# A plan of norm steps for each token block between two layers, and a budget for VectorE's weight conversions

## The chip, the cores and the metric

The kernel runs on one core of one Trainium2 chip. The metric is the device time of one execution in microseconds (us), taken from runs without the profiler; the profile comes from one further execution. Engines are named TensorE (PE in the profile, its weight loads PEld), VectorE (DVE), ScalarE (ACT), GpSimd (POOL) and SyncE (SP, which only issues DMAs here).

## The reference, cut to what matters

Attention over 4 batches, 8 heads, 576 positions and 64 channels, with a learned position bias, gives x of 2304 tokens x 512. Two feed-forward layers follow; the weights arrive as float64.

```python
def _moe_ref(x, w_in, w_out):                 # layer 1, d_ff 2048
    h = x @ w_in
    g = h * np.cos(h)
    return g @ w_out

def _moe2_ref(x, w_gate, w_val, w_out, rms_g):  # layer 2, d_ff 1536
    rms = np.sqrt(np.mean(x * x, axis=-1, keepdims=True) + 1e-06)
    xn = x / rms * rms_g
    g = xn @ w_gate
    silu = g * (1.0 / (1.0 + np.exp(-g)))
    val = xn @ w_val
    return silu * val @ w_out
```

## The kernel before, in words

Attention fills the first 300 us of the profile and is not touched. Then come 140 **items**, numbered n = 0 to 139: 0 to 79 are layer 1, 80 to 139 layer 2. An item is one token block times one slice of 128 hidden units. The tokens lie in five blocks, four of 512 tokens (0, 1, 3, 4) and one of 256 (block 2). Layer 1 has four chunks of four slices, layer 2 four chunks of three; inside a chunk the loop runs over blocks, then slices. In the last chunk of layer 1 (items 60 to 79) and the first of layer 2 (80 to 94) the blocks come in the order 0, 2, 1, 3, 4, so layer 1 ends for block 0 at item 63, block 2 at 67, block 1 at 71, block 3 at 75, block 4 at 79, and layer 2 starts them at items 80, 83, 86, 89 and 92.

Each fp32 product is done as three matmuls of a high and a low part (high x high, high x low, low x high). `run_item(n)` issues in this order: squares and output steps of the norm that are due (ScalarE, GpSimd); the product up of item n (12 matmuls into a PSUM tile `h`, `hg` or `hv`; three such tiles rotate, and the norm's transposes `ssp` and `rbp` use the same three); the activation; the product down of item n-2 (`item_down`, matmuls into `y`, which has five PSUM tiles, four for a block of 512); a tick of the weight pipeline. In layer 1 the activation is three VectorE steps (L653 to L655), Abs and Sin on ScalarE, one VectorE step (L662), a cast on ScalarE (L663) and a subtraction on GpSimd (L664), the last two making the high and low part of `g`, which the product down of item n reads two items later. In layer 2 it is Sigmoid on ScalarE, two VectorE steps (L676, L679), then the cast and the subtraction (L680, L681). When `item_down` ends a chunk of a block, VectorE moves its four `y` tiles to `yacc` (L715, L717: below, the evictions); in two places of the order (`sums_first`) they stand ahead of L662.

Weights pass a pipeline of pieces (512 columns each, two per slice in layer 1, three in layer 2): a DMA of float64, an absolute value on ScalarE (L113), four VectorE operations that make float32 of it (L124, L126, L128, L130: **quarters**; `w_conv` counts them), then a split into high and low (ScalarE L148, GpSimd L149) into a ring of ten. Piece i is called split i below. A split waits until the ring's slot is free, and the number of splits in a tick is one in layer 1 and two in layer 2.

Between the layers each block is normalised: squares (`rms_sq`), three additions of them on VectorE (`rms_add`, L733), a sum by transposes on TensorE (`rms_sum`, L739), the reciprocal root (`rms_mean`: four VectorE operations, L748 to L752, and twelve small GpSimd operations, L754 to L757), transposes back (`rms_back`, L764) and a copy, the multiplication of four parts (`rms_xn`, VectorE L771), and the split into `xh` and `xl` (`rms_out`, ScalarE L776 and GpSimd L777). All engines work through their instructions in program order, so the item at which a step is issued sets what stands behind it.

Of the kernel before, what the change touches and what calls it, by code (L numbers as in the profile page):

```python
# [25 lines left out]
BLKS = [(0, 512), (512, 512), (2048, 256), (1024, 512), (1536, 512)]  # L26
# [3 lines left out]
CH1 = 4  # L30
CH2 = 3
# [7 lines left out]
LAG = 2  # L39
# [5 lines left out]

SMALLPS = {33, 34, 35}
LB = {10: 0, 11: 1, 18: 2, 19: 3, 26: 4, 27: 5}
WF = 2
ORDER2 = [0, 2, 1, 3, 4]

LEAST = 2.0 ** -15
# [3 lines left out]
def attn_moe(tc, qd, kd, vd, smallp, lrow, ident_d, wf1, wf2, rmsg, out):  # L55
# [61 lines left out]
    def w_conv(quarters=2):  # L117
        for _ in range(quarters):
            i = wstate["conv"]
            r = raw_t[i]  # L120
            hi, lo = r[:, :, 1], r[:, :, 0]
            t = w32_t[i]
            if wstate["half"] == 0:
                nc.vector.tensor_scalar(t.bitcast(F32), t.bitcast(F32), LEAST, GREATEST, op0=ALU.max, op1=ALU.min)  # L124
            elif wstate["half"] == 1:
                nc.vector.tensor_scalar(t, t, 3, 0x3FFFFFFF, op0=ALU.logical_shift_left, op1=ALU.bitwise_and)  # L126
            elif wstate["half"] == 2:
                nc.vector.scalar_tensor_tensor(t, hi, -0x40000000, t, op0=ALU.bitwise_and, op1=ALU.bitwise_or)  # L128
            else:
                nc.vector.scalar_tensor_tensor(t, lo, 29, t, op0=ALU.logical_shift_right, op1=ALU.bitwise_or)  # L130
                raw_t.pop(i)
                wstate["conv"] += 1
            wstate["half"] = (wstate["half"] + 1) % 4

    def w_split(eng=nc.gpsimd):
# [13 lines left out]
        eng.tensor_tensor(t[:, 1, :], r, t[:, 0, :].bitcast(F32), op=ALU.subtract)  # L149
        w_t[pieces[i]] = t  # L150
        wstate["split"] += 1

    def w_fill(halves=1):
        for _ in range(halves):
            if wstate["conv"] < wstate["absd"]:
                w_conv()

    def w_tick(can_split, nsplit=1, forward=True):

# [304 lines left out]
    small = ph0.tile([128, 34 + NTT + NR], F32, name="small")  # L464
# [119 lines left out]
    items = []  # L584
# [7 lines left out]
    NI = len(items)  # L592
# [35 lines left out]
    def tasks(n, fns):  # L628
        k = 0
        for fn, *a in later.get(n, ()):  # L630
            if fn in fns:
                fn(*a)
                k += 1
        return k

    def fill(n):
        return tasks(n, (rms_add, rms_mean, rms_xn))

    def item_up(n, between=None, sums_first=False):
        m, c, bi, fi = items[n]  # L640
        t0, tn = BLKS[bi]
        f = c * (CH1 if m == 1 else CH2) + fi
        g = mp.tile([128, 2, 512], F32R, tag="g", name="g", bufs=LAG + 2)
        if n == 0:
            mp.tile([128, 96], F32, name="evenm")
        if m == 1:
            ps = up(w_t[(1, f, 0)], bi, "h")[:, :tn]
            if between is not None:
                between()
            tasks(n, (rms_sum, rms_back))  # L650
            t = mp.tile([128, 512], F32, tag="t", name="t", bufs=2)[:, :tn]
            r = mp.tile([128, 512], F32, tag="r", name="r", bufs=2)[:, :tn]
            nc.vector.tensor_scalar(t, ps, INV2PI, MAGIC, op0=ALU.mult, op1=ALU.add)  # L653
            nc.vector.tensor_scalar(t, t, MAGIC, -TWO_PI, op0=ALU.subtract, op1=ALU.mult)  # L654
            nc.vector.tensor_tensor(r, ps, t, op=ALU.add)  # L655
            if fill(n) < WF:
                w_fill()
            nc.scalar.activation(r, r, AF.Abs)  # L658
            nc.scalar.activation(r, r, AF.Sin, bias=halfpi[:, 0:1], scale=-1.0)

            def end():
                nc.vector.tensor_tensor(t, r, ps, op=ALU.mult)  # L662
                nc.scalar.copy(g[:, 0, :tn], t)  # L663
                nc.gpsimd.tensor_tensor(g[:, 1, :tn], t, g[:, 0, :tn].bitcast(F32), op=ALU.subtract)  # L664


            if sums_first:
                gt[n] = g
                return end
            end()  # L670
        else:
            pg = up(w_t[(2, f, 0)], bi, "hg")[:, :tn]
            tasks(n, (rms_sum, rms_back))
            t = mp.tile([128, 512], F32, tag="t", name="t", bufs=2)[:, :tn]
            nc.scalar.activation(t, pg, AF.Sigmoid)  # L675
            nc.vector.tensor_tensor(t, t, pg, op=ALU.mult)  # L676
            fill(n)
            pv = up(w_t[(2, f, 1)], bi, "hv")[:, :tn]
            nc.vector.tensor_tensor(t, t, pv, op=ALU.mult)  # L679
            nc.scalar.copy(g[:, 0, :tn], t)  # L680
            nc.gpsimd.tensor_tensor(g[:, 1, :tn], t, g[:, 0, :tn].bitcast(F32), op=ALU.subtract)  # L681
        gt[n] = g

    def item_down(n):
        m, c, bi, fi = items[n]
        t0, tn = BLKS[bi]
        ch = CH1 if m == 1 else CH2
        nch = (NF1 if m == 1 else NF2) // ch
        f = c * ch + fi
        g = gt.pop(n)  # L690
        wt = w_t[(m, f, 1 if m == 1 else 2)]
        nd = 4 if m == 1 else tn // 128
        wid = tn if m == 1 else 512
        if fi == 0:
            ypsum[bi] = [env["psY"].tile([128, 512], F32, tag="y", name="y", bufs=5) for _ in range(nd)]
        for d in range(nd):
            ps = ypsum[bi][d][:, :wid]
            w_ = (wt[:, 0, 128 * d:128 * d + 128], wt[:, 1, 128 * d:128 * d + 128], g[:, 0, :tn], g[:, 1, :tn])
            if m == 1:
                mm3(ps, [w_], tn, fi == 0, fi == ch - 1)  # L700
            else:
                gs = slice(128 * d, 128 * d + 128)
                mm3(ps, [(g[:, 0, gs], g[:, 1, gs], wt[:, 0, :], wt[:, 1, :])], 512, fi == 0, fi == ch - 1)
        if fi == ch - 1:
            acc = yacc if m == 1 else oacc
            if c == 0:
                if tn == 512:
                    acc[bi] = env["yp"].tile([128, 4, 512], F32, tag="y", name="yacc", bufs=4)
                else:
                    acc[bi] = env["yp"].tile([128, nd, wid], F32, tag="ys", name="yaccs", bufs=1)  # L710
            a = acc[bi]
            for d in range(nd):
                ps = ypsum[bi][d][:, :wid]
                if c == 0:
                    nc.vector.tensor_copy(a[:, d, :wid], ps)  # L715
                else:
                    nc.vector.tensor_tensor(a[:, d, :wid], ps, a[:, d, :wid], op=ALU.add)  # L717
                if m == 2 and c == nch - 1:
                    nc.sync.dma_start(out[t0 + 128 * d:t0 + 128 * d + 128, :], a[:, d, :])
            if m == 1 and c == nch - 1:  # L720
                return bi
        return None

    rst = {}

# [47 lines left out]
    def rms_out(bi, d):  # L773
# [3 lines left out]
        nc.gpsimd.tensor_tensor(xl[:, d, t0:t0 + tn], t, xh[:, d, t0:t0 + tn].bitcast(F32), op=ALU.subtract)  # L777

    NI1 = NF1 * len(BLKS)
    RMS_AT = (-14, -10, -5, -1, 2)  # L780
    RMS_STEPS = [
        [(rms_sq, 0), (rms_sq, 1)], [(rms_add, 1), (rms_sq, 2), (rms_sq, 3)], [(rms_add, 2), (rms_add, 3)],
        [(rms_sum,), (rms_mean,)], [], [(rms_back,)], [(rms_xn, 0)],
        [(rms_xn, 1), (rms_xn, 2), (rms_out, 0)], [(rms_xn, 3), (rms_out, 1)], [(rms_out, 2), (rms_out, 3)],
    ]
    def ready(i):
        while wstate["split"] <= i:
            if wstate["split"] < wstate["conv"]:
                w_split()
            elif wstate["conv"] < wstate["abs"]:  # L790
                w_conv()
            elif wstate["abs"] < wstate["dma"]:
                w_abs()
            else:
                w_dma()

    def run_item(n, between=None):
        tasks(n, (rms_sq, rms_out))
        end = None
        if n < NI:  # L800
            m, c, bi, fi = items[n]
            ready(pieces.index((m, c * (CH1 if m == 1 else CH2) + fi, m - 1)))
            end = item_up(n, between, n >= LAG and items[n - LAG][3] == CH1 - 1 and 2 in (bi, items[n - LAG][2]))
        d = n - LAG
        if d >= 0:
            m, c, bi, fi = items[d]
            ready(pieces.index((m, c * (CH1 if m == 1 else CH2) + fi, m)))
            bi = item_down(d)
            if bi is not None:
                n0 = NI1 + RMS_AT[ORDER2.index(bi)]  # L810
                for i, x in enumerate(RMS_STEPS):
                    later.setdefault(n0 + i, []).extend((x_[0], bi, *x_[1:]) for x_ in x)
        if end is not None:
            end()
        m, c, bi, fi = items[min(n, NI - 1)]
        w_tick(lambda i: i < WA + WB or n > 1 and (i < RING or lastuse[pieces[i - RING]] <= n - SPL),
               nsplit=2 if n < 6 or m == 2 else 1)
        if m == 2:
            w_fill(2 if n % 2 else 1)

    def rest():
        av(15, 1)
# [89 lines left out]
```

## Time and profile before

| | |
|---|---|
| median of 3 runs | 1155.5 us (1155.28 to 1155.86) |
| profiled execution | 1155.4 us, span 1153.6 us |
| PE busy | 1142.8 us (99%) |
| PEld busy | 919.0 us (80%) |
| DVE busy | 806.9 us (70%) |
| ACT busy | 546.5 us (47%) |
| POOL busy | 443.8 us (38%) |
| granted TensorE clock | 1.000 over the span |

The span runs from the first to the last instruction; 1.8 us of the execution lie outside it. A share is of the whole span, so an engine with a low share can still be full in one stretch. Matmuls are pipelined and their ends are modelled: the time from one start to the next tells more than the time of one.

### The profile page before, as it was taken

Reading aid. Unit: us, or ns where it says so; the run is one execution under the profiler, and the core shown is the slowest. Engines: PE = TensorE matmul, PEld = TensorE weight load, DVE = VectorE, ACT = ScalarE, POOL = GpSimd, SP = SyncE. Lnnn points to the kernel's source line nnn. Section 1 sums busy time; section 2 is a strip of 40 time slices with the busy share of each in tenths; the row PEclk is TensorE's granted clock in tenths of the full one; section 3 lists DMA queues with packets and bytes.
Section 4 is the critical chain, followed back from the end, with each engine's and each line's share of the span. In section 5 each row is a group of like instructions: output and inputs, shape, how many; then the busy total and the mean of one; then the engine's idle time right before and its main releaser. Section 6 shows DMA issues by size and latency. Waiting matters only on the chain.

```text
span 1153.6 us, 18552 instructions
## 1 busy us (share of the span) xinstructions
PE 1142.8 (99%) x6982; PEld 919.0 (80%) x6982; DVE 806.9 (70%) x1527; ACT 546.5 (47%) x1105; POOL 443.8 (38%) x554
## 2 busy tenths in 40 slices
PE   9999999999999999999999999999999999999998
PEld 4477777777788888888888878888888888888887
DVE  8866888888797798698789897874555355543232
ACT  8877888887644444454445545332322222222111
POOL 0244576665242442253244356743421242133111
PEclk9999999999999999999999999999999999999999
DMA  8825343442010011011101101210111011100111
GB/s 255 285 81 170 101 155 121 161 143 72 28 49 34 19 55 56 19 45 63 39 20 56 35 19 31 62 55 19 55 56 55 1 55 55 55 1 1 37 60 69
DMA packets 30715, 79.28 MB, mean 69 GB/s; under 512 B 3873, under 2 KB 4129, under 8 KB 30625
## 3 DMA queue, kind: packets, MB, share of 16 engines
q1 hardware_dynamic: 30480, 77.80, 21.4%
q8 instruction: 55, 0.90, 0.3%
q14 instruction: 36, 0.29, 0.1%
q10 hardware_dynamic: 144, 0.29, 0.1%
HBM read 62.47 MB, written 15.61 MB: 68 GB/s over the span
## 4 chain that ended last, share of the span: by engine, by line
PE 87%; DVE 8%; ACT 3%; issue 1%; ACTq 0%; DVEq 0%
PE y L614 25%; PE h L614 14%; PE hg L614 12%; PE hv L614 12%; PE psS L245 7%; PE o L325 7%; PE pt L282 6%; PE psb L541 3%; DVE yacc L717 1%; PE pt L290 1%; DVE t L654 1%; DVE sq L733 1%; DVE r L655 1%; DVE w L130 1%; DVE w L128 1%
## 5 line engine op out<-in xcount | busy, mean ns | idle before, releaser
L664 POOL TENSOR_TENSOR g<-t,g 128x512 fp32r<-128x512 f32 (+1 forms) x80 | 98.0, 1224 | 235.5 <-ACT g L663 235.5
L681 POOL TENSOR_TENSOR g<-t,g 128x512 fp32r<-128x512 f32 (+1 forms) x60 | 74.7, 1245 | 291.7 <-ACT g L680 291.7
L676 DVE TENSOR_TENSOR t<-t,hg 128x512 f32<-128x512 f32 (+1 forms) x60 | 38.0, 633 | 138.5 <-ACT t L675 138.5
L614 PE MATMUL y<-g,wB 128*128 128x512 f32 (+1 forms) x600 | 133.0, 370 | 1.2 <-DVE yacc L717 1.2
L259 DVE CUSTOM_DVE_ANT_0 e<-psS,bias 128x576 f32<-128x576 f32 x144 | 103.9, 754 | 40.2 <-PE psS L245 36.1
L614 PEld LDWEIGHTS y<-g,wB 128*128 128x128 f32 x600 | 104.9, 188 | 21.2 <-DVE yacc L717 2.5
L268 ACT ACTIVATE e<-e,sm 128x576 f32<-128x576 f32 x144 | 112.0, 778 | 6.4 <-DVE sm L259 5.6
L675 ACT ACTIVATE t<-hg 128x512 f32<-128x512 f32 (+1 forms) x60 | 33.3, 554 | 167.6 <-PE hg L614 161.3
L680 ACT CAST g<-t 128x512 fp32r<-128x512 f32 (+1 forms) x60 | 34.7, 578 | 164.0 <-DVE t L679 164.0
L614 PE MATMUL h<-xh,wB 128*128 128x512 f32 (+1 forms) x360 | 109.1, 369 | 0.0
L614 PE MATMUL hg<-xh,wB 128*128 128x512 f32 (+1 forms) x320 | 96.9, 368 | 0.4 <-DVE t L676 0.4
L658 ACT ACTIVATE r<-r 128x512 f32<-128x512 f32 (+1 forms) x80 | 47.1, 589 | 105.9 <-DVE r L655 105.4
L614 PE MATMUL hv<-xh,wB 128*128 128x512 f32 (+1 forms) x320 | 97.1, 369 | 0.0
L663 ACT CAST g<-t 128x512 fp32r<-128x512 f32 (+1 forms) x80 | 46.2, 578 | 96.3 <-DVE t L662 90.4
L614 PE MATMUL y<-wB,g 128*128 128x512 f32 x378 | 91.4, 389 | 0.0
L325 PE MATMUL o<-eT,v 128*64 128x256 f32 (+1 forms) x640 | 83.9, 408 | 0.0
L614 PEld LDWEIGHTS y<-wB,g 128*128 128x128 f32 x378 | 70.5, 188 | 14.3
L614 PE MATMUL y<-g,wC 128*128 128x512 f32 (+1 forms) x360 | 79.9, 370 | 0.1
L245 PE MATMUL psS<-kt,qt 64*128 64x288 f32 (+1 forms) x810 | 79.5, 309 | 0.0
L679 DVE TENSOR_TENSOR t<-t,hv 128x512 f32<-128x512 f32 (+1 forms) x60 | 38.0, 633 | 58.3 <-PE hv L614 58.0
L245 PEld LDWEIGHTS psS<-kt,qt 64*128 64x128 f32 (+1 forms) x810 | 61.9, 185 | 20.6 <-issue 13.2
L614 PEld LDWEIGHTS h<-xh,wB 128*128 128x128 f32 x360 | 65.8, 189 | 12.2 <-issue 0.5
(142 smaller groups left out, 2639.8 us busy)
## 6 DMA issues: line engine op xcount, KB each, us to landing
raw<-in_wf_dram SPq DMA_DIRECT2D x68, 512.0 KB, 3.6
bdram<-G SPq DMA_DIRECT2D x36, 295.5 KB, 4.7
bias<-bdram SPq DMA_DIRECT2D x32, 288.0 KB, 3.7
v<-in_vd_dram SPq DMA_DIRECT2D x16, 320.0 KB, 3.5
rawk<-in_kd_dram SPq DMA_DIRECT2D x15, 320.0 KB, 4.5
rawq<-in_qd_dram SPq DMA_DIRECT2D x15, 320.0 KB, 3.0
out_dram<-yacc SPq DMA_DIRECT2D x16, 256.0 KB, 2.1
bias<-bdram SPq DMA_DIRECT2D x4, 144.0 KB, 2.9
```

The costliest lines, as they stand in the source:

```text
L245: nc.tensor.matmul(ps[:, x, 0:288], qt[r, a, 128 * p:128 * p + 128], kt[r, b_, k0:k0 + 288], start=(n == 0), stop=(n == len(terms) - 1), t ...
L259: nc.vector.tensor_tensor_reduce(out=e.rearrange("p (a b) -> p a b", a=2), in0=ps[:, :, 0:288], in1=bias_t[j].rearrange("p (a b) -> p a b" ...
L268: nc.scalar.activation(e, e, AF.Exp, bias=s_["m"][:, j:j + 1], scale=-1.0, accum_out=s_["sum"][:, j:j + 1])
L282: nc.tensor.transpose(pt[:, 128 * i:128 * i + 128], e[:, k0:k0 + 128], ident)
L325: nc.tensor.matmul(o[64 * hh:64 * hh + 64, 0:n], vt[:, c, 64 * hh:64 * hh + 64], eT[:, 2 * c + (hh if c < 4 else 0), :], start=(c == 0), s ...
L614: nc.tensor.matmul(ps, a, b_, start=(first and k == 0), stop=(last and k == tot - 1))
L658: nc.scalar.activation(r, r, AF.Abs)
L663: nc.scalar.copy(g[:, 0, :tn], t)
L664: nc.gpsimd.tensor_tensor(g[:, 1, :tn], t, g[:, 0, :tn].bitcast(F32), op=ALU.subtract)
L676: nc.vector.tensor_tensor(t, t, pg, op=ALU.mult)
L679: nc.vector.tensor_tensor(t, t, pv, op=ALU.mult)
L681: nc.gpsimd.tensor_tensor(g[:, 1, :tn], t, g[:, 0, :tn].bitcast(F32), op=ALU.subtract)
```

## The change

Before, every block ran the same ten norm steps, one item apart, from a start that differed by block (`RMS_AT`). Now each block has a plan of its own (`RMS_PLAN`), with offsets from item 80. Block 0: the multiplications stand at items 72, 74 and 75 (were 72 to 74). Block 2: sum at 74 (was 73), back at 76 (75), multiplications at 78 and 79 (76 to 78), outputs at 79 and 80 (77 to 79). Block 1: all squares at 75, all additions at 76. Block 3: all squares at 79, all additions at 80, sum and mean at 81 (82), back at 83 (84). Block 4 stays.

The quarters go by a budget. Before, a layer-1 item issued two of them (none where two or more norm steps stood on VectorE), a layer-2 item four or two by turns. Now `w_quarters(n)` reckons room in tenths of a microsecond, takes off the norm steps of the item and the evictions, and issues up to four: four in a full item of layer 1, two in a small one, none where four full tiles are evicted, and up to four at the end of a layer-2 item. How many pieces may be in flight stays as it was, so the same quarters are issued earlier, in denser groups.

```diff
-WF = 2
...
     def fill(n):
-        return tasks(n, (rms_add, rms_mean, rms_xn))
+        return tasks(n, (rms_add, rms_mean)) + tasks(n, (rms_xn,))
+
+    def w_quarters(n):
+        m, c, bi, fi = items[n]
+        small = BLKS[bi][1] < 512
+        room = (28 if small else 53) - (14 if small else 25) if m == 1 else (42 if small else 80) - (8 if small else 12)
+        for fn, b, *a in later.get(n, ()):
+            room -= {rms_add: 7, rms_mean: 11, rms_xn: 8}.get(fn, 0) * (0.6 if BLKS[b][1] < 512 else 1)
+        if n >= LAG:
+            m, c, bi, fi = items[n - LAG]
+            if fi == (CH1 if m == 1 else CH2) - 1:
+                room -= (16 if m == 1 else 12) if BLKS[bi][1] < 512 else 24
+        for _ in range(max(0, min(4, int(room / 6.5)))):
+            if wstate["conv"] < wstate["absd"]:
+                w_conv(1)
...
             nc.vector.tensor_tensor(r, ps, t, op=ALU.add)
-            if fill(n) < WF:
-                w_fill()
+            fill(n)
+            w_quarters(n)
...
-    RMS_AT = (-14, -10, -5, -1, 2)
-    RMS_STEPS = [
-        [(rms_sq, 0), (rms_sq, 1)], [(rms_add, 1), (rms_sq, 2), (rms_sq, 3)], [(rms_add, 2), (rms_add, 3)],
-        [(rms_sum,), (rms_mean,)], [], [(rms_back,)], [(rms_xn, 0)],
-        [(rms_xn, 1), (rms_xn, 2), (rms_out, 0)], [(rms_xn, 3), (rms_out, 1)], [(rms_out, 2), (rms_out, 3)],
+    SQ, ADD, SUM, BACK, XN, OUT = range(6)
+    RMS_PLAN = [
+        {-14: [(SQ, 0), (SQ, 1)], -13: [(ADD, 1), (SQ, 2), (SQ, 3)], -12: [(ADD, 2), (ADD, 3)], -11: [(SUM,)], -9: [(BACK,)],
+         -8: [(XN, 0)], -7: [(OUT, 0)], -6: [(XN, 1)], -5: [(XN, 2), (XN, 3), (OUT, 1)], -4: [(OUT, 2), (OUT, 3)]},
+        {-10: [(SQ, 0), (SQ, 1)], -9: [(ADD, 1), (SQ, 2), (SQ, 3)], -8: [(ADD, 2), (ADD, 3)], -6: [(SUM,)], -4: [(BACK,)],
+         -2: [(XN, 0), (XN, 1)], -1: [(XN, 2), (XN, 3), (OUT, 0), (OUT, 1)], 0: [(OUT, 2), (OUT, 3)]},
+        {-5: [(SQ, 0), (SQ, 1), (SQ, 2), (SQ, 3)], -4: [(ADD, 1), (ADD, 2), (ADD, 3)], -2: [(SUM,)], 0: [(BACK,)],
+         1: [(XN, 0)], 2: [(XN, 1), (XN, 2), (OUT, 0)], 3: [(XN, 3), (OUT, 1)], 4: [(OUT, 2), (OUT, 3)]},
+        {-1: [(SQ, 0), (SQ, 1), (SQ, 2), (SQ, 3)], 0: [(ADD, 1), (ADD, 2), (ADD, 3)], 1: [(SUM,)], 3: [(BACK,)],
+         5: [(XN, 0)], 6: [(XN, 1), (XN, 2), (OUT, 0)], 7: [(XN, 3), (OUT, 1)], 8: [(OUT, 2), (OUT, 3)]},
+        {2: [(SQ, 0), (SQ, 1)], 3: [(ADD, 1), (SQ, 2), (SQ, 3)], 4: [(ADD, 2), (ADD, 3)], 5: [(SUM,)], 7: [(BACK,)],
+         8: [(XN, 0)], 9: [(XN, 1), (XN, 2), (OUT, 0)], 10: [(XN, 3), (OUT, 1)], 11: [(OUT, 2), (OUT, 3)]},
     ]
...
-        if m == 2:
-            w_fill(2 if n % 2 else 1)
+        if m == 2 and n < NI:
+            w_quarters(n)
```

## Rows read from the trace of the kernel before

**Rows 1.** Busy time by stretch (windows): PE, PEld, DVE, ACT, POOL, granted clock, DMA.

```profile
300.00:600.00 300.00, 300.00 (x1465) 251.65 (x1465) 246.21 (x391) 139.12 (x231) 106.66 (x83) 1.00 0.13 39
600.00:750.00 150.00, 145.96 (x728) 121.91 (x727) 131.01 (x214) 73.51 (x135) 81.33 (x112) 1.00 0.14 39
```

**Rows 2.** The chain that ended last, one piece: start, length, what.

```profile
578.50 2.72 PE y L614 x12
```

**Rows 3.** Timeline of TensorE, 613 to 741 us: start, length, what, idle ahead.

```profile
613.75 0.28 PE L614 MATMUL h<-xh,wB 128*128 128x256 f32 x1
...
615.18 2.91 PE L614 MATMUL y<-g,wC 128*128 128x512 f32 x12
...
625.09 1.82 PE L614 MATMUL y<-g,wB 128*128 128x256 f32 x9 [1.03 <-DVE yacc L717]
...
637.27 0.66 PE L739 MATMUL ssp<-ident,sq 128*128 128x128 f32 x4 [0.17 <-DVE sq L733]
...
687.67 0.66 PE L739 MATMUL ssp<-ident,sq 128*128 128x128 f32 x4 [0.63 <-DVE sq L733]
...
732.25 2.79 PE L614 MATMUL y<-wA,g 128*128 128x512 f32 x11 [1.00 <-POOL wA L149]
...
740.84 0.50 PE L614 MATMUL hg<-xh,wB 128*128 128x512 f32 x1 [0.44 <-DVE t L676]
```

**Rows 4.** Timeline of VectorE at item 65.

```profile
622.77 1.66 DVE L130 SCALAR_TENSOR_TENSOR w<-raw,w 128x512 int32<-128x512 int32 x1
624.36 2.47 DVE L717 TENSOR_TENSOR yacc<-y,yacc 128x512 f32<-128x512 f32 x4
```

**Rows 5.** Timeline of VectorE at items 73 and 77.

```profile
664.72 2.47 DVE L717 TENSOR_TENSOR yacc<-y,yacc 128x512 f32<-128x512 f32 x4
...
685.67 1.95 DVE L733 TENSOR_TENSOR sq<-sq 128x512 f32<-128x512 f32 x2
```

**Rows 6.** Timeline of GpSimd at items 81 and 82.

```profile
715.06 1.30 POOL L149 TENSOR_TENSOR wC<-w,wC 128x512 fp32r<-128x512 f32 x1
...
722.62 0.20 POOL L754 TENSOR_TENSOR rsm<-rsm 128x4 f32<-128x4 f32 x1 [4.56 <-DVE rsm L752]
...
726.88 0.53 POOL L757 TENSOR_TENSOR rsm<-rsm 128x4 f32<-128x4 f32 x1
727.36 1.30 POOL L681 TENSOR_TENSOR g<-t,g 128x512 fp32r<-128x512 f32 x1
```

**Rows 7.** Timeline of VectorE, the first step of block 3's mean.

```profile
721.25 0.68 DVE L748 TENSOR_REDUCE rsm<-ssp 128x4 f32<-128x512 f32 x1
```

**Rows 8.** Timeline of TensorE, starts of products of items 81 and 82.

```profile
705.14 0.39 PE L614 MATMUL hg<-xh,wB 128*128 128x512 f32 x1
...
716.38 0.48 PE L614 MATMUL hv<-xh,wC 128*128 128x512 f32 x1
```

**Rows 9.** Timeline of VectorE: quarters alone and beside GpSimd.

```profile
696.32 0.68 DVE L128 SCALAR_TENSOR_TENSOR w<-raw,w 128x512 int32<-128x512 int32 x1
...
715.39 1.52 DVE L128 SCALAR_TENSOR_TENSOR w<-raw,w 128x512 int32<-128x512 int32 x1
716.94 1.67 DVE L130 SCALAR_TENSOR_TENSOR w<-raw,w 128x512 int32<-128x512 int32 x1
718.53 0.41 DVE L124 TENSOR_SCALAR w<-w 128x512 f32<-128x512 f32 x1
```

**Rows 10.** Timeline of ScalarE, two squares of block 3.

```profile
700.62 1.15 ACT L729 ACTIVATE sq<-yacc 128x512 f32<-128x512 f32 x2
```

**Rows 11.** Timeline of VectorE at item 80.

```profile
704.18 0.69 DVE L676 TENSOR_TENSOR t<-t,hg 128x512 f32<-128x512 f32 x1 [4.69 <-ACT t L675]
```

**Rows 12.** Timeline of VectorE, item 25 of layer 1.

```profile
424.31 0.69 DVE L653 TENSOR_SCALAR t<-h 128x512 f32<-128x512 f32 x1 [0.82 <-PE h L614]
...
428.88 2.47 DVE L717 TENSOR_TENSOR yacc<-y,yacc 128x512 f32<-128x512 f32 x4
```

**Rows 13.** Timeline of TensorE, the first product down of block 1's chunk.

```profile
429.48 2.88 PE L614 MATMUL y<-g,wC 128*128 128x512 f32 x12
```

More of the change, by code (lines that the diff above doesn't have):

```diff
@@ L151, in w_split @@
         wstate["split"] += 1
[L153 to L156, printed above, removed]
     def w_tick(can_split, nsplit=1, forward=True):
@@ L719, in item_down @@
                     nc.sync.dma_start(out[t0 + 128 * d:t0 + 128 * d + 128, :], a[:, d, :])
-            if m == 1 and c == nch - 1:
-                return bi
-        return None
     rst = {}
@@ L779, in attn_moe @@
     NI1 = NF1 * len(BLKS)
-    RMS_AT = (-14, -10, -5, -1, 2)
-    RMS_STEPS = [
-        [(rms_sq, 0), (rms_sq, 1)], [(rms_add, 1), (rms_sq, 2), (rms_sq, 3)], [(rms_add, 2), (rms_add, 3)],
-        [(rms_sum,), (rms_mean,)], [], [(rms_back,)], [(rms_xn, 0)],
-        [(rms_xn, 1), (rms_xn, 2), (rms_out, 0)], [(rms_xn, 3), (rms_out, 1)], [(rms_out, 2), (rms_out, 3)],
-    ]
+    SQ, ADD, SUM, BACK, XN, OUT = range(6)
[10 more added lines that the diff above has]
+         8: [(XN, 0)], 9: [(XN, 1), (XN, 2), (OUT, 0)], 10: [(XN, 3), (OUT, 1)], 11: [(OUT, 2), (OUT, 3)]},
+    ]
+    RMS_FNS = [(rms_sq,), (rms_add,), (rms_sum, rms_mean), (rms_back,), (rms_xn,), (rms_out,)]
+    for bi, plan in zip(ORDER2, RMS_PLAN):
+        for at, todo in plan.items():
+            for k, *d in todo:
+                later.setdefault(NI1 + at, []).extend((fn, bi, *d) for fn in RMS_FNS[k])
     def ready(i):
@@ L807, in run_item @@
             ready(pieces.index((m, c * (CH1 if m == 1 else CH2) + fi, m)))
[L808 to L812, printed above, removed]
+            item_down(d)
         if end is not None:
```

## The prediction

> **What bounds the kernel now.** I read the windows by stretch first, since the shares of the whole span mix stages. From 300 to 600 us TensorE is busy without a gap; from 600 to 750 us, where layer 1 hands over to layer 2, it is idle for 4.0 us, and VectorE is busy for 131 of 150 us [rows 1]. The granted clock is 1.00 in both stretches, which is the level of 2.4 GHz, so no clock enters the sum. TensorE therefore sets the time, and only what stands between two matmuls can be saved. The chain of waits gives its steady pace: twelve matmuls of 512 columns, one product, in 2.72 us [rows 2]; twelve of 256 columns take 1.43, from 613.75 to 615.18 [rows 3].
>
> Then the timeline of TensorE shows seven gaps, 1.03, 0.17, 0.18, 0.63, 1.00, 0.46 and 0.44 us, 3.91 together; five of them stand in [rows 3], and the 0.18 (an eviction) and the 0.46 (a sum) look like their neighbours. Each costs more than its idle time, since the first matmuls behind a gap run slower than the pace. The whole loss comes from counting. Between the starts at 613.75 and 740.84, 127.1 us, stand 35 products of 512 columns (95.2), 14 of 256 (20.1), one half product (1.4) and the transposes of nine norm steps. Four transposes behind a gap take 0.66 [rows 3]; at the pace I put seven such groups at 0.45 and two of half the size at 0.23, 3.6. That is 120.3, so 6.8 us are lost; 6.7 is what I count on. This is the most the change can win, and the profiled execution would then be at 1155.4 - 6.7 = 1148.7. Its 1155.4 lies 0.1 under the median of the runs, so the sum needs no shift.
>
> **The old gaps, one by one.** The reader is to see who stands in front on VectorE. At item 65 a quarter of 1.66 us begins at 622.77, so the evictions start at 624.36 and the next product down waits 1.03 [rows 3, 4]. The budget gives item 65 nothing (14 tenths of room less 24), so the evictions start when their product ends, some 2 us earlier; this gap goes. At item 73 the evictions start only at 664.72 [rows 5], behind two multiplications, a mean and an activation step; the plan moves the first three to items 74 and 75, and 0.18 goes. At item 77 the last additions of block 1 end at 687.62 (1.95 for two, beside GpSimd [rows 5]) and the sum waits 0.63 [rows 3]; the additions move to item 76, an item's time (two products, 5.4) ahead of need. The gap at 637.27 is of 0.17, and one quarter of 0.41 or more [rows 9] falls away ahead of its additions: gone. The 1.00 at 732.25 is split 40, issued at item 83 in front of a product of item 84 [rows 3]; its quarters now end at item 80, so it is issued at item 82: gone. The last two gaps follow four quarters at the end of item 83, the first two of which would now be left, and none at 84: gone. So 6.7, if nothing takes their place.
>
> **What the change adds.** Squares, additions, multiplications, outputs, quarters and DMAs are the same in number; a DMA of weights follows its piece's last quarter, so SyncE issues some earlier, in a stretch where the DMA share is 0.14 [rows 1], at no cost. What is new is order, in four places.
>
> First place, item 80. Item 81's first product needs the PSUM tile that L676 of item 80 reads. That step ended at 704.87 [rows 11], 0.27 before TensorE came to it at 705.14 [rows 8]. ScalarE now has two more squares of block 3 ahead of item 79's sine, 1.15 us [rows 10], and a weight step more ahead of the sigmoid, which I put at half of that, 0.6; two outputs of the small block take the place of two squares behind the sine, 0.4 less: 1.3 in all. VectorE, with the two additions that took 1.95 [rows 5] gone from item 77, is about 1.7 earlier there; TensorE comes about 1.0 sooner, without the 0.63 and its restart. Margin 0.27 - 1.3 + 1.7 - 1.0 = -0.3, with the restart a loss of 0.5 (0 to 1.3, the whole of ScalarE's extra).
>
> Second place, items 81 and 82, the dear one. GpSimd works in program order, and the mean of block 3 moves from item 82 to 81, ahead of that item's g and of split 39. Split 39 now ends at 716.36 [rows 6], and item 82's second product, whose third matmul needs it, starts at 716.38 [rows 8]: 0.5 to spare. After, from the end E of item 80's L676: three additions at 0.68 (like the quarter of two inputs in [rows 9]) 2.0, L679 0.7, four quarters, L676 of item 81 0.7, the mean's VectorE part 1.37 (721.25 to 722.62 [rows 6, 7]), its twelve GpSimd operations, g 1.30 and the split 1.30 [rows 6]. The quarters: alone 0.41 or 0.68 each, 2.2 for four; beside GpSimd two of them took 1.52 and 1.67 [rows 9], and GpSimd has g and two splits just then, so I take 1.52 + 1.67 + 2 x 0.41 = 4.0. The twelve: 4.74 in the row (722.62 to 727.36 [rows 6]), or 2.4 if each were the first's 0.20; I take 4.2, near the row. Sum 15.6. TensorE comes to the third matmul at E + 0.1 + 2.72 + 0.45 + 3 x 2.72 + 0.45 = 11.9. Late by 3.7; consecutive starts overlap by some 0.08, so 3.5. From both sides: quarters alone and a chain of 3.3 give 0.9; quarters of 6.1, each of three behind a whole GpSimd operation of 1.30, and 4.74 give 6.1.
>
> On that last bound a page speaks. The rows show a quarter of 0.68 taking 1.52 beside a GpSimd subtraction of 1.30 [rows 6, 9]. The Trainium skill, page "SBUF — State Buffer", section "Who interferes with whom", says that VectorE and GpSimd share a pair of ports as an exclusive lock, and whichever comes second is blocked for the whole instruction. By the rule at full a group of four would wait behind every GpSimd operation and the stall would be 6.1; by the rows, 3.5.
>
> Third place, the chunks of layer 1. At item 25 the evictions start at 428.88 and the first of four is out 0.62 later [rows 12]; the product down that follows starts at 429.48 and needs that tile for its second quarter, at 430.16 [rows 13], so 0.66 is spare. Items 22, 23 and 24 now have four quarters instead of two: six more at a mean of 0.55 [rows 9], 3.3, less 0.5 of the 0.82 that VectorE waited for its input at item 25 [rows 12], and item 25's own two, 1.7 with one of them blocked, are gone. The evictions come 1.1 later: 0.5 lost with the restart, once here and once at item 45. If half of the six met GpSimd like the blocked ones in [rows 9], it would be 1.2 each; if VectorE slips in first, nothing. So 1.0 (0 to 2.4). In items 26 to 34 no split runs and I see room. In the chunks of layer 2 VectorE waits for ScalarE, 4.69 us in [rows 11], and four quarters in place of three cost nothing there; if that cover were gone, a quarter is 0.4 to 1.7.
>
> Fourth, the denser steps at items 66 to 79, 0.3 (0 to 1.5): the additions of block 0 end, by my count, 0.2 to 0.4 before they are needed.
>
> Sum: -6.7 + 0.5 + 3.5 + 1.0 + 0.3 = -1.4, so 1154.0.
>
> **Rivals.** *The new stall is small.* If VectorE's quarters at item 80 slip in between GpSimd's work, item 81's L676 follows its sigmoid at once, the stall at item 82 is about 1, and layer 1 keeps its margins: -6.7 + 0.5 + 1 + 0.7 = -4.5, 1150.9. For it speaks that quarters of 0.41 occur just behind blocked ones [rows 9]; against it, GpSimd has three large operations in that stretch.
>
> *Too dense: slower.* In groups of four, every quarter finds a GpSimd operation running and waits for its end, as the two blocked ones of [rows 9] did. The place is item 80 and items 22 to 24 of each chunk. At item 82 that costs 6.1; in layer 1 an item needs four activation steps of some 0.6 [rows 12], 2.4, and 2.2 + 2 x 1.3 = 4.8 for quarters behind two GpSimd operations, 7.2 against TensorE's 5.44 (two products, [rows 2]), 1.8 late in each of three, less 0.66 and the 1.7 that item 25 saves: 3.0, twice. Sum -6.7 + 0.5 + 6.1 + 6.0 + 0.3 = +6.2, 1161.6; with one of the two places at the full price, +2 to +4. It decides from about four quarters in 5 us on. Against it: blocked and free ones stand side by side in the rows.
>
> *It doesn't do what it says.* VectorE's work in the handover is the same, 131 of 150 us [rows 1]; gaps removed at one step appear at the next, and the time stays at 1155.4, within 1.
>
> **How the numbers follow.** The forecast has 0.50, with its losses at 3.2 to 7.5: 1151.9 to 1156.2. The small stall has 0.25 (1149.8 to 1151.9), too dense 0.13 (1157.4 to 1161.6), no effect 0.12 (1154.4 to 1156.4). A measurement can tell about 0.2%, 2.3 us, from no change, so faster means under 1153.2. Faster: 0.25 and some 0.4 of the forecast, 0.45. Slower: 0.13. Same: the remaining 0.42. The range, 1150.4 to 1157.6, leaves out a part of the small stall and nearly all of too dense.
>
> **What would show it.** Right: no gap at items 65, 73, 77 and none before split 40; a new one in front of item 82's third matmul of the second product, released by GpSimd's split, of 2 to 5 us; small ones at evictions of items 25 and 45; the mean of block 3 on GpSimd ahead of that split. Wrong: if that gap is under 1 us the kernel is near 1151; if waits for evictions recur in every chunk of layer 1, it is slower than before.

## The result, and the profile after

The changed kernel takes 1161.63 us in the median of 6 runs (1161.27 to 1163.06) against 1155.39 for the kernel before on the same chip: a ratio of 1.0057, 95% interval 1.0046 to 1.0068. It is 6.2 us slower; the prediction was 1154.0, with a range that ended at 1157.6. The profiled execution took 1162.45 us, 7.05 above that of before. Its lines carry other numbers: matmuls L608, quarters L123 to L129, evictions L723 and L725, the step that was L662 is L670, those that were L676 and L679 are L684 and L687, the mean's GpSimd operations L759 to L762.

First the windows of the changed kernel (columns as in [rows 1]); the two short ones lie around item 82.

```profile
300.00:600.00 300.00, 298.14 (x1450) 248.87 (x1451) 232.91 (x388) 137.27 (x228) 103.24 (x83) 1.00 0.13 39
722.00:724.00 2.00, 0.00 (x0) 0.00 (x0) 2.00 (x2) 0.00 (x0) 2.00 (x3) 0.66 0.83 258
724.00:728.00 4.00, 3.96 (x9) 3.14 (x10) 0.54 (x1) 0.00 (x0) 1.68 (x1) 0.50 0.01 2
600.00:750.00 150.00, 143.65 (x711) 120.51 (x710) 126.70 (x209) 73.12 (x134) 79.18 (x102) 0.98 0.12 36
```

Layer 1, which had no gap [rows 1], is now idle for 1.86 us, and the handover for 6.35 instead of 4.04. From 724 to 728 us the granted clock is 0.50, the level of 1.2 GHz. The next two fences are TensorE's waits in the changed kernel (tile, line, releaser: us, times, longest), of 300 to 600 us and of 600 to 750 us.

```profile
PE y L608 <- DVE yacc L725: 1.4, 2, 0.8
PE y L608 <- POOL g L672: 0.3, 1, 0.3
PE y L608 <- DVE yacc L723: 0.2, 1, 0.2
```

```profile
PE hv L608 <- POOL wC L148: 3.7, 1, 3.7
PE hv L608 <- DVE t L670: 1.5, 1, 1.5
PE y L608 <- POOL g L672: 1.2, 2, 0.9
```

None of the seven old gaps [rows 3] is among them; whether all of them went as foreseen is taken up below. What came has four places. I measure a loss below as the distance of two matmul starts less the usual one there. It is more than the wait, which in these views is idle time alone, because the first matmuls behind a gap are slower (the restart).

**Item 82.** TensorE and GpSimd of the changed kernel, timeline:

```profile
719.94 0.39 PE L608 MATMUL hv<-xl,wC 128*128 128x512 f32 x1
724.04 1.22 PE L608 MATMUL hv<-xh,wC 128*128 128x512 f32 x2 [3.72 <-POOL wC L148]
725.06 0.63 PE L608 MATMUL hv<-xl,wC 128*128 128x512 f32 x1
```

```profile
711.64 1.36 POOL L689 TENSOR_TENSOR g<-t,g 128x512 fp32r<-128x512 f32 x1 [3.81 <-ACT g L688]
712.97 3.17 POOL L148 TENSOR_TENSOR wC<-w,wC 128x512 fp32r<-128x512 f32 x2
716.88 0.63 POOL L759 TENSOR_TENSOR rsm<-rsm 128x4 f32<-128x4 f32 x1 [0.74 <-DVE rsm L757]
...
720.38 0.72 POOL L762 TENSOR_TENSOR rsm<-rsm 128x4 f32<-128x4 f32 x1
721.06 1.26 POOL L689 TENSOR_TENSOR g<-t,g 128x512 fp32r<-128x512 f32 x1
722.28 1.70 POOL L148 TENSOR_TENSOR wC<-w,wC 128x512 fp32r<-128x512 f32 x1
```

The twelve operations of block 3's mean run from 716.88 to 721.06, then g, then split 39 until 723.98; the third matmul of the second product starts at 724.04. Against [rows 6, 8], where the split had 0.5 to spare, TensorE loses 3.88 us. Behind it the next matmuls cost more: 1.02 us for two, where the usual step is 0.23 each. Counted by starts, that adds up to 2.6 us until the steps are the usual ones again at 729.63.

**Item 80.** ScalarE, VectorE and TensorE of the changed kernel, a fence each:

```profile
698.55 2.19 ACT L734 ACTIVATE sq<-yacc 128x512 f32<-128x512 f32 x4
700.65 0.61 ACT L666 ACTIVATE r<-r 128x512 f32<-128x512 f32 x1
701.30 0.72 ACT L667 ACTIVATE r<-r,halfpi 128x512 f32<-128x512 f32 x1
```

```profile
702.05 0.69 DVE L670 TENSOR_TENSOR t<-r,h 128x512 f32<-128x512 f32 x1 [0.63 <-ACT r L667]
```

```profile
702.79 0.50 PE L608 MATMUL hv<-xh,wB 128*128 128x512 f32 x1 [1.47 <-DVE t L670]
```

Four squares (two in [rows 10]) stand ahead of item 79's Abs and Sin. L670 of item 79 reads its PSUM tile `h` after them, and with three tiles in rotation and one taken by block 1's `rbp`, the second product of item 80 needs that very tile: 1.72 us are lost, 1.75 with the restart, one product earlier than the place that the prediction watched [rows 8, 11]. VectorE had also worked off a blocked quarter of 1.67 us ahead of L670, but that ended 0.6 before the sine did.

**Layer 1.** VectorE of the changed kernel at items 23 to 25, where the kernel before issued two quarters an item:

```profile
416.32 0.69 DVE L663 TENSOR_TENSOR r<-h,t 128x512 f32<-128x512 f32 x1
416.93 0.80 DVE L123 TENSOR_SCALAR w<-w 128x512 f32<-128x512 f32 x1
417.76 1.40 DVE L125 TENSOR_SCALAR w<-w 128x512 int32<-128x512 int32 x1
419.19 0.69 DVE L127 SCALAR_TENSOR_TENSOR w<-raw,w 128x512 int32<-128x512 int32 x1
...
420.53 0.68 DVE L670 TENSOR_TENSOR t<-r,h 128x512 f32<-128x512 f32 x1
...
422.31 0.69 DVE L663 TENSOR_TENSOR r<-h,t 128x512 f32<-128x512 f32 x1
...
428.30 0.69 DVE L663 TENSOR_TENSOR r<-h,t 128x512 f32<-128x512 f32 x1
430.45 0.69 DVE L670 TENSOR_TENSOR t<-r,h 128x512 f32<-128x512 f32 x1 [1.45 <-ACT r L667]
431.05 1.28 DVE L725 TENSOR_TENSOR yacc<-y,yacc 128x512 f32<-128x512 f32 x2
```

From one L663 to the next VectorE needs 5.99 us twice running, TensorE 5.44 (two products, [rows 2]): in these two items, with four quarters of which one is blocked, VectorE is the slower engine. The evictions start at 431.05, 0.67 after the product down that needs their tiles (430.38); in [rows 12, 13] they were 0.60 ahead of it. Counted start by start over the stretch from 300 to 600 us, TensorE loses 3.3 us more than before: 0.84 at item 25, 1.08 at item 45 and 2.0 in six smaller places, three of them in the first chunk, less 0.6 that the kernel before lost in this stretch.

**Products down at items 65 and 76.** Both wait for GpSimd's g, the last two waits in the list: 1.1 us behind four quarters at item 63, 0.6 behind block 2's mean, whose twelve GpSimd operations took 5.4 us.

### The profile page after: what moved, and what is told of

Same layout as the page of the kernel before. It is cut to its first block, busy times and chain, and to the rows that moved or that the text cites. A ratio compares the mean times of both kernels' runs of the same rounds, so it can differ in the third digit from the quotient of the medians.

```text
span 1160.7 us, 18641 instructions
## 1 busy us (share of the span) xinstructions
PE 1145.6 (99%) x6982; PEld 920.8 (79%) x6982; DVE 798.7 (69%) x1527; ACT 546.4 (47%) x1105; POOL 439.5 (38%) x554
## 4 chain that ended last, share of the span: by engine, by line
PE 84%; DVE 9%; ACT 4%; issue 2%; POOL 1%; DMA 1%; ACTq 0%; DVEq 0%; POOLq 0%
PE y L608 24%; PE hv L608 12%; PE h L608 12%; PE hg L608 12%; PE psS L239 7%; PE o L319 7%; PE pt L276 5%; PE psb L535 2%; DVE t L670 1%; DVE t L662 1%; DVE r L663 1%; DVE yacc L725 1%; DVE t L661 1%; PE pt L284 1%; DVE w L125 1%
## 5 line engine op out<-in xcount | busy, mean ns | idle before, releaser
L672 POOL TENSOR_TENSOR g<-t,g 128x512 fp32r<-128x512 f32 (+1 forms) x80 | 98.2, 1228 | 239.3 <-ACT g L671 239.3
L689 POOL TENSOR_TENSOR g<-t,g 128x512 fp32r<-128x512 f32 (+1 forms) x60 | 71.3, 1188 | 303.7 <-ACT g L688 303.7
L608 PE MATMUL y<-g,wB 128*128 128x512 f32 (+1 forms) x600 | 133.4, 370 | 1.3 <-POOL g L672 1.1
L684 DVE TENSOR_TENSOR t<-t,hg 128x512 f32<-128x512 f32 (+1 forms) x60 | 37.9, 631 | 131.1 <-ACT t L683 131.1
L608 PEld LDWEIGHTS y<-g,wB 128*128 128x128 f32 x600 | 104.5, 188 | 22.0 <-POOL g L672 2.6
L608 PE MATMUL h<-xh,wB 128*128 128x512 f32 (+1 forms) x360 | 109.1, 369 | 0.0
L608 PE MATMUL hv<-xh,wB 128*128 128x512 f32 (+1 forms) x320 | 97.3, 369 | 1.5 <-DVE t L670 1.5
L608 PE MATMUL hg<-xh,wB 128*128 128x512 f32 (+1 forms) x320 | 96.8, 368 | 0.0
L608 PE MATMUL y<-wB,g 128*128 128x512 f32 x378 | 91.9, 391 | 0.0
L670 DVE TENSOR_TENSOR t<-r,h 128x512 f32<-128x512 f32 (+1 forms) x80 | 50.4, 630 | 50.7 <-ACT r L667 50.1
L608 PEld LDWEIGHTS y<-wB,g 128*128 128x128 f32 x378 | 71.0, 189 | 14.6
L608 PE MATMUL y<-g,wC 128*128 128x512 f32 (+1 forms) x360 | 80.6, 370 | 1.7 <-DVE yacc L725 1.4
L687 DVE TENSOR_TENSOR t<-t,hv 128x512 f32<-128x512 f32 (+1 forms) x60 | 38.0, 633 | 55.6 <-PE hv L608 55.6
```

What stands on the lines that cost most here:

```text
L608: nc.tensor.matmul(ps, a, b_, start=(first and k == 0), stop=(last and k == tot - 1))
```

## The experiments

All edits are against the changed kernel unless said otherwise. Ratios are to the kernel before.

**Back with the sum.** Block 3's sum, mean and transposes back go to items 82 and 84, as before.

```diff
-        {-1: [...], 0: [...], 1: [(SUM,)], 3: [(BACK,)],
+        {-1: [...], 0: [...], 2: [(SUM,)], 4: [(BACK,)],
```

> One step of the plan undone: block 3's sum and mean at item 82 instead of 81, its transposes back at 84 instead of 83. Theory A (the mean's twelve GpSimd operations stand ahead of split 39, and the clock falls behind the gap): the gap of 3.7 us in front of item 82's third matmul and the stretch at half clock behind it go together, 6.5 us, to about 1155.0. Theory B (the quarters are too dense, VectorE is late at item 81 whatever stands on GpSimd): item 81's L676 step stays as late, split 39 still ends 1 us or more late, and the time falls by 3 us at most, to 1158.5 or more.

1158.23 us, 1.0026 [1.0016, 1.0037]. The loss at item 82 falls from 3.88 to 0.47, and the granted clock stays at 1.00. Losses of 0.68 and 0.94 appear at item 84 and at block 4's sum; the wait at the sum, among TensorE's waits:

```profile
PE ssp L744 <- DVE sq L738: 0.8, 1, 0.8
```

**The other way round: split earlier.** Three splits in the tick of item 80, so split 39 stands ahead of the mean.

```diff
-               nsplit=2 if n < 6 or m == 2 else 1)
+               nsplit=3 if n == NI1 else 2 if n < 6 or m == 2 else 1)
```

> The changed kernel with three splits instead of two in the weight tick of item 80, so that split 39 stands on GpSimd ahead of the mean of block 3 and of item 81's g; nothing else moves. Theory A: the gap and the half clock go, 6.5 us, to about 1155.0, with the mean where the change put it. Theory B: VectorE's lateness at item 81 shows at the next product instead, and 2 us or more of a gap remain between items 81 and 84: 1157 or more.

1158.85 us, 1.0031 [1.0019, 1.0043]. The wait at item 82 is gone; a new one stands at block 4's sum. First TensorE's waits of this kernel from 600 to 750 us, then its VectorE ahead of that sum.

```profile
PE ssp L744 <- DVE sq L738: 2.4, 1, 2.4
PE hv L608 <- DVE t L670: 1.4, 1, 1.4
```

```profile
725.99 0.67 DVE L687 TENSOR_TENSOR t<-t,hv 128x512 f32<-128x512 f32 x1
728.45 0.53 DVE L123 TENSOR_SCALAR w<-w 128x512 f32<-128x512 f32 x1 [1.78 <-ACT w L112]
729.01 1.41 DVE L125 TENSOR_SCALAR w<-w 128x512 int32<-128x512 int32 x1
730.45 1.66 DVE L127 SCALAR_TENSOR_TENSOR w<-raw,w 128x512 int32<-128x512 int32 x1
...
739.25 2.14 DVE L738 TENSOR_TENSOR sq<-sq 128x512 f32<-128x512 f32 x2
```

VectorE stands idle for 1.78 us for a quarter whose piece has no absolute value yet, then works four of them off, with the norm queued behind. The two runs agree that mean and split collide on GpSimd, and that a relieved handover shows the next wait: of the 6.5 us that the first theory gave, they bring back 3.4 and 2.8.

**One half of the change at a time.** First the new plan with the old rule for quarters, then the old norm steps with the new budget.

```diff
...
-            fill(n)
-            w_quarters(n)
+            if fill(n) < 2:
+                w_fill()
...
-        if m == 2 and n < NI:
-            w_quarters(n)
+        if m == 2:
+            w_fill(2 if n % 2 else 1)
```

> The new plan of norm steps with the old rule for quarters (two per item of layer 1, four or two by turns in layer 2). Theory A: split 39 still stands behind the mean, so a gap at item 82 stays, less the two quarters at item 80 that are now fewer (1.0 to 2.0 us less): 1 to 2.7 us with a clock that may hold; the small gaps in the chunks of layer 1 (4.4 us together) go back to 0.65: 1151 to 1155. Theory B: with the old quarters the gap at item 82 is gone altogether and all that is left is the wait at item 80: 1150 to 1151.

> The old steps of the norm, ten in a row per block, with the new budget of quarters. Theory A: no gap in front of item 82's second product, since the mean stays at item 82; the small gaps of layer 1 come (3.8 us more than before) and two old gaps go (item 65's eviction, split 40), 3 us: 1155 to 1158, clock at full. Theory B: the quarters alone make most of the loss: 1159 or more, with a gap of 2 us or more near item 81 or 82.

Plan alone: 1158.80 us, 1.0033 [1.0022, 1.0044]. TensorE is busy for 300.00 us of 300 to 600, so layer 1's waits belong to the budget. The loss at item 82 stays at 3.70, with two quarters at item 80 instead of four, so both theories missed. But it is made up otherwise. Under the old rule the piece of split 39 gets its last quarters only at the end of item 80, the split is issued an item later, and on GpSimd it stands behind an output step of item 82 as well as behind the mean:

```profile
717.78 1.44 POOL L787 TENSOR_TENSOR xl<-yacc,xh 128x512 fp32r<-128x512 f32 x1
719.18 1.70 POOL L148 TENSOR_TENSOR wC<-w,wC 128x512 fp32r<-128x512 f32 x1
```

Without that step, 1.4 us, some 2.3 would be lost (an estimate from these lines). So the mean ahead of the split costs TensorE with dense quarters and without them; what the dense quarters add to the changed kernel's 3.88 no run takes alone.

Budget alone: 1161.20 us, 1.0049 [1.0034, 1.0064], with layer 1's waits, 1.40 lost at item 82 and 2.41 at item 84. The second theory's time came, but its gap stands at item 84, a wait of 2.16, and the clock, which the first theory had at full, is 0.51 from 736.8 to 740.2 us behind it. Either half alone is slower than the kernel before, and the budget is the dearer one.

**Filling the gap.** Twelve more matmuls stand ahead of item 82's second product, in the same PSUM tile; what waits for split 39 is unchanged.

```diff
+        for _ in range(warm):
+            nc.tensor.matmul(ps[:, :tn], wt[:, 0, 0:128], xh[:, 0, t0:t0 + tn], start=True, stop=True)
...
-            pv = up(w_t[(2, f, 1)], bi, "hv")[:, :tn]
+            pv = up(w_t[(2, f, 1)], bi, "hv", 12 if n == 82 else 0)[:, :tn]
```

> The changed kernel with twelve more matmuls of 512 columns (2.7 us of work whose result is overwritten) ahead of item 82's second product, so that TensorE works through most of the 3.7 us in which it would wait for split 39. Theory A (the idle stretch itself lets the granted clock fall, and the half clock behind it costs up to 2.7 us): the split ends as before, the product starts as before, no stretch at half clock, and the kernel is 1 to 2.7 us faster with more work, 1159 to 1160.6. Theory C (the clock falls for another reason, or its fall costs nothing): the same time as the changed kernel or later, 1161.6 to 1164.

1160.04 us, 1.0041 [1.0028, 1.0053]: with more work it is 1.6 us faster. The timeline of its TensorE, then its windows:

```profile
719.79 2.88 PE L615 MATMUL hv<-xh,wC 128*128 128x512 f32 x12
...
724.12 0.73 PE L608 MATMUL hv<-xh,wC 128*128 128x512 f32 x2 [0.99 <-POOL wC L148]
```

```profile
722.00:724.00 2.00, 1.12 (x5) 0.58 (x4) 2.00 (x3) 0.00 (x0) 2.00 (x2) 1.00 0.84 254
724.00:728.00 4.00, 3.88 (x17) 3.23 (x18) 1.30 (x2) 0.56 (x2) 1.76 (x2) 1.00 0.01 4
```

The third matmul starts at 724.12, as late as in the changed kernel (724.04), but the clock stays at 1.00 and 17 matmuls instead of 9 fit into the next 4 us. So the 1.6 us is what the half clock behind the gap costs.

**Block 3 as before.** Its squares, additions, sum and transposes back all as in the kernel before.

```diff
-        {-1: [(SQ, 0), (SQ, 1), (SQ, 2), (SQ, 3)], 0: [(ADD, 1), (ADD, 2), (ADD, 3)], 1: [(SUM,)], 3: [(BACK,)],
+        {-1: [(SQ, 0), (SQ, 1)], 0: [(ADD, 1), (SQ, 2), (SQ, 3)], 1: [(ADD, 2), (ADD, 3)], 2: [(SUM,)], 4: [(BACK,)],
```

> The changed kernel with block 3's steps as before the change (two squares at 79, two at 80, additions at 80 and 81, sum at 82, back at 84); the budget and the other blocks stay. Against the kernel with only the sum put back, this tells what the four squares ahead of item 79's sine cost. Theory A: the wait of 1.7 at item 80's second product falls to 0.4 or less as with the old plan, 1156.5 to 1157. Theory B (quarters of item 79 hold the step that it waits for): the wait stays above 1 us, 1158.

1158.67 us, 1.0028 [1.0018, 1.0039]. The loss at item 80 falls from 1.72 to 1.00 only, that at item 82 to 1.47. Both theories hold a part of item 80: with two squares the sine ends earlier, and now the blocked quarter of item 79 is what holds L670. In the runs below that have two squares and no quarter at item 79, 0.7 is lost there.

**Fewer quarters everywhere.** On top of the last edit, once the old rule for quarters throughout (none where the evictions stand first), once a cap of two quarters an item in all of layer 1.

```diff
-        for _ in range(max(0, min(4, int(room / 6.5)))):
+        for _ in range(max(0, min(2 if items[n][0] == 1 else 4, int(room / 6.5)))):
```

> The new plan for blocks 0, 2 and 1, block 3 as before the change, the old rule for quarters, and none where the evictions stand ahead of L670 (items 65 and 69, and their like in earlier chunks). Theory A: nothing of the new losses is left and most of the old gaps are gone: 1150 to 1151.5, faster than both. Theory B (gaps only move from step to step): 1154 to 1156.

> As the kernel with block 3's old steps and the new budget, but with at most two quarters in an item of layer 1 (up to four stay in layer 2). Theory A (groups of four make the evictions of layer 1 late): the waits at items 5, 9, 25 and 45, 3.5 us together, fall under 1 us in all, and the wait at item 63 goes: 1151.5 to 1153.5. Theory B (what costs in layer 1 is the placing of quarters, not their number): 1155 or more.

The first theory missed in both: 1162.86 us, 1.0066 [1.0053, 1.0080], and 1164.40 us, 1.0076 [1.0063, 1.0088], with a mean granted clock of 0.993 to 0.997. TensorE's waits in the first of them, 600 to 750 us:

```profile
PE y L613 <- ACT wA L147: 3.7, 1, 3.7
PE hg L613 <- ACT wC L147: 2.3, 1, 2.3
PE hg L613 <- POOL wC L148: 1.2, 1, 1.2
PE y L613 <- POOL wA L148: 1.0, 1, 1.0
```

Now the pieces themselves come too late for item 82, and the half clock follows these waits too. The supply of converted weights up to piece 40 is just in time; the next run, which keeps the budget from item 56 on, has no such wait.

**Old rule before item 56, budget from there.**

```diff
...
-            fill(n)
-            w_quarters(n)
+            k = fill(n)
+            if n >= 56:
+                w_quarters(n)
+            elif k < 2:
+                w_fill()
```

> The changed kernel with the old rule for quarters up to item 55 and the budget from there on. Theory A (groups of four quarters beside GpSimd's work make VectorE late in every chunk of layer 1, where the pieces were in time anyway): the waits of items 1 to 55, 3.9 us together, go back to the 0.5 of before; nothing later moves: 3.4 us less, 1158.2. Theory B (the waits of layer 1 cost nothing in the end, since the handover absorbs them): within 1 us of the changed kernel's 1161.6.

1158.27 us, 1.0023 [1.0013, 1.0033], 3.4 less than the changed kernel. Its window of layer 1 has the gaps gone:

```profile
300.00:600.00 300.00, 299.98 (x1465) 251.71 (x1465) 245.61 (x392) 138.72 (x230) 106.18 (x83) 1.00 0.13 39
```

**The repairs together.** That edit, split 39 at item 80, and caps on the budget (two quarters at item 63, one at 74, none at 79 and 83); once with block 3 as before, once with block 3 as in the change.

> The changed kernel with each loss taken away by itself: old rule for quarters up to item 55; at most two quarters at item 63, one at 74, none at 79 and 83; block 3's steps as before the change; three splits in the tick of item 80. Pieces are still converted as early as with the budget. Theory A: waits of some 1 us in all are left in layer 1's end, 1149.5 to 1151.5, faster than both kernels. Theory B (the gaps move): 1154 or more.

> The same, but with block 3's steps as the change puts them (four squares at item 79, sum and mean at 81). With split 39 ahead of the mean, theory A says that only the four squares ahead of item 79's sine are left: a wait of 0.7 to 1.4 us at item 80, so 0.5 to 1.2 us above the run with block 3's old steps, 1150 to 1152.5. Theory B (the early mean costs GpSimd and VectorE elsewhere): 2 us or more above it.

1157.61 us, 1.0017 [1.0008, 1.0026], and 1155.83 us, 1.0002 [0.9993, 1.0011]: the first theory missed in both. In the first run, VectorE waits 1.77 us for an absolute value at item 82, works four quarters until 728.9, and block 3's transposes back come late by 2.6, item 84's second product by 1.9. Those four belong to piece 42, which like piece 41 is not needed before item 95.

**No quarter at items 81 to 85.** The cap 0 there as well, in both kernels, and in the changed kernel with the moved split as the only other edit.

```diff
-        for _ in range(max(0, min(4, int(room / 6.5)))):
+        for _ in range(max(0, min({63: 2, 74: 1, 79: 0, 81: 0, 82: 0, 83: 0, 84: 0, 85: 0}.get(n, 4), int(room / 6.5)))):
```

> The tuned kernel with block 3's steps as before, but with no quarter issued at items 81 to 85 (piece 41, the next one, is first needed at item 95). Theory A (what is left in the handover comes from quarters that VectorE holds in front of the activation steps of items 82 to 84 while their piece's absolute value on ScalarE is still to come): the gaps of 2.58 and 1.86 us at items 83 and 84 fall under 0.5 each, time 1157.6 - 5.0 = about 1152.5 (1151 to 1153.5). Theory B (the work of VectorE in the handover is simply too much, waits move to the next step): other gaps of the same sum appear from item 84 on, time 1156 or more.

> The same with block 3's steps as in the changed kernel. Theory A: the gaps at items 83, 84 and at block 4's sum (1.23, 0.92 and 2.0 us) go, the gap of 1.9 us at item 80 behind ScalarE's four squares stays; time 1155.8 - 3.5 = about 1152.3 (1151 to 1153.5). Theory B: 1155 or more, with new gaps behind item 84.

> The changed kernel with two edits alone: split 39 issued at item 80, and no quarter at items 81 to 85. Layer 1 and the rest stay as changed. The split alone gave 1158.85 and left a gap of 2.52 us at block 4's sum. Theory A: that gap goes and time falls by some 2.5 to 3.5 to about 1155.8 (1155 to 1156.5). Theory B: no fall, 1158 or more.

1151.50 us, 0.9965 [0.9951, 0.9979]; 1151.89 us, 0.9968 [0.9956, 0.9981]; 1156.18 us, 1.0006 [0.9997, 1.0014]. TensorE's waits from 600 to 750 us, of the first and of the third:

```profile
PE hv L613 <- DVE t L695: 0.6, 1, 0.6
PE hv L613 <- DVE t L678: 0.5, 1, 0.5
PE y L613 <- DVE yacc L733: 0.3, 1, 0.3
```

```profile
PE hv L608 <- DVE t L670: 1.5, 1, 1.5
PE y L608 <- POOL g L672: 1.1, 2, 0.9
```

The gaps did not move on. The first theory holds: what was left came from quarters that stood in VectorE's order ahead of their data. The first of the three beats the kernel before by 3.8 us, with VectorE busy for 124.84 us of 600 to 750, where before it was 131.01 [rows 1]. Its block 3 runs as before and that of the second as changed, and the two times agree within 0.4: the new plan of block 3 itself makes no difference that these runs can tell once split and quarters are out of its way.

## Why the prediction was wrong

The steps that missed by most are the clock, which entered the sum with nothing (2.6 in the profiled execution), and layer 1 (3.3 for 1.0); items 80 and 65 to 76 add 1.25 and 1.4.

**The old gaps, -6.7: the size right, the last two by luck.** All seven are gone in the changed kernel. But the prediction overlooked the budget's four quarters at item 82, ahead of block 4's additions, and that VectorE would stand idle there for an absolute value:

```profile
731.18 0.54 DVE L123 TENSOR_SCALAR w<-w 128x512 f32<-128x512 f32 x1 [1.77 <-ACT w L112]
```

Nobody waits for them only because TensorE itself is late by the stall at item 82. In the two runs without that stall 0.94 and 2.5 us are lost at block 4's sum, where the kernel before had its gap of 0.46. That gap went for good only with no quarters at items 81 to 85, in the version that is 3.8 faster than before.

**Item 82, +3.5: right.** 3.88, in the chain that was written down: additions, L687, quarters, L684, mean, g, split; from the end of item 80's L684 (708.26) to the end of the split 15.7 us, where the sum had 15.6. Two of the four quarters cost 1.40 and 1.66 (the prediction took 1.67 and 1.52), and the twelve small operations with their tail 4.2. The blocked quarter L125 ran from 711.89 to 713.29, beside the g that ran from 711.64 to 713.00. The Trainium skill, page "SBUF — State Buffer", section "Who interferes with whom", has the engine that comes second wait for the whole instruction of the other; the trace agrees: from 300 us on, the 23 quarters L125 that started while a GpSimd operation of 512 columns ran took 1.39 to 1.41, the other 34 took 0.42 to 0.43. But two of the four met one, not all, so the upper bound was not reached.

**Layer 1, +1.0 (0 to 2.4): mis-sized, 3.3.** The step that failed is "six more at a mean of 0.55", and with it "once here and once at item 45". At items 23 and 24 a group of four took 3.6 (416.93 to 420.53) and 3.5 where that mean gives 2.2, since one quarter in each is blocked; only the group at item 22 took 2.25. With a blocked one an item of VectorE takes 5.99 against 5.44, so the delay grows with each such item: items 25 and 45 lose 0.84 and 1.08 instead of 0.5 each. And the sum named only these two places, where eight lose, some without an eviction. Taking these quarters away gave back 3.4 (1161.63 to 1158.27, with the old rule before item 56).

**Item 80, +0.5 (0 to 1.3): mis-sized, 1.75, and at another product.** The sum followed L676's tile to item 81, and overlooked that item 80's second product takes the tile of item 79, whose last reader waits for ScalarE's sine behind the four squares. With two squares the loss is still 1.00, for then the blocked quarter holds that step; without it, 0.7.

**Items 66 to 79, +0.3 (0 to 1.5): 0.6, and 1.1 beside it.** 0.6 at item 76, GpSimd's g behind a mean. The 1.1 at item 65, a g behind four quarters, was in no term: there the prediction looked at the evictions only. The additions of block 0, which I feared for, were in time.

**"No clock enters the sum": wrong.** It read the clock of a kernel whose longest gap was 1.03, and did not ask what the gap of 2 to 5 us that it forecast would do to it. Behind the new gap of 3.72 the clock was 0.50, and counted by starts the matmuls lost 2.6 in the profiled execution; 1.6 is what the filled gap gave back in the median, 2.45 between the two profiled executions.

By these counts the profiled execution is explained: -6.8 + 3.3 + 1.1 + 0.6 + 1.75 + 3.9 + 2.6 = 6.45, of 7.05. Two small losses beside them, 0.21 at 611.76 and 0.27 at 631.05, leave 0.1.

The rival "too dense" named the right direction, and of the sign that the prediction gave for it, waits for evictions in every chunk of layer 1, three chunks of four show it. That it came to 1161.6, the measured time, is luck: item 82 lost 3.9 and not 6.1, layer 1 3.3 and not 6.0; the clock and item 80 made up the rest. The prediction had a blocked quarter's price in its rows and used it at item 82, and a mean of free quarters for layer 1: had one quarter in four been taken as blocked there, 2.2 + 1.0 = 3.2 and the activation's 2.4 would have made 5.6 an item, over TensorE's 5.44, and waits in every chunk would have been in sight.

What stays open: how layer 1's loss divides among the six smaller places, which no run takes one by one, and how much of the 3.88 at item 82 the dense quarters make.

## What to carry to other kernels

Reckon an added group of operations against the pace of one item, with the blocked durations that the trace shows beside the other engine, not against the mean: an engine that is 0.5 us over the pace loses in every item until something lets it catch up. Work that is not due soon should not be issued ahead of work that is: here five items without conversions, whose piece was needed ten or more items later, were worth 2.7 to 6.1 us, while fewer conversions in the items before, whose pieces were due, cost 4.2 and 5.7. And when a wait is moved, look for a long gap's second price, the clock behind it.

## What the runs showed of the hardware

The half clock does not follow every such gap. In the profiled execution with the plan alone TensorE waited 3.53 us at item 82 and the granted clock stayed at 1.00, as this window of it shows; over its eight executions the mean granted clock went from 1.000 (1157.18 us, the profiled one) to 0.996 (1160.69 us).

```profile
720.00:730.00 10.00, 9.06 (x53) 8.09 (x54) 7.48 (x10) 3.62 (x7) 3.62 (x3) 1.00 0.18 52
```

In the changed kernel it was 0.997 to 0.999 in all six. Nor does the length of the wait alone decide: in the profiled execution of the budget alone 0.51 followed a wait of 2.16 us (736.8 to 740.2 us), in that with the split moved a wait of 2.35 left the clock at 1.00 (741 to 745 us). A stall therefore costs a varying time beyond itself, 2.6 us in the profiled execution of the changed kernel.
